# An S4 layer with MLP on one core: the tables of exponentials and sines built in one phase, or in two phases, one for each half of the channels

## The chip, the cores and the metric

The kernel runs on one core of one Trainium2 chip. It is written in Bass, with SBUF and PSUM addresses and the order of all instructions set by the kernel itself. The metric is the device time of one execution in microseconds (us). PE is TensorE, ACT is ScalarE, DVE is VectorE, POOL is GpSimd, and SP is the engine whose queue issues most of the DMAs.

## The reference

The input is u, 2048 positions by 512 channels, in bf16. An S4 layer with 128 complex states for each channel is followed by an MLP with 1376 hidden columns.

```python
# S4 part, on x = LN(u)
dt = exp(log_dt)[:, None]                      # 512 x 1
A, Bc, Cc = A_re + 1j*A_im, B_re + 1j*B_im, C_re + 1j*C_im   # 512 x 128
P = exp((dt*A)[:, :, None] * l)                # l = 0 .. 2047, rounded to bf16
K = einsum("dn,dnl,dn->dl", Cc, P, dt*Bc).real # one kernel of 2048 taps per channel
y = irfft(rfft(pad(x)) * rfft(pad(K)))[:2048] + x * Dskip
h = u + y
# MLP part
out = h + gelu_tanh(LN(LN(h)) @ w1 + b1) @ w2 + b2
```

The two layer norms in the MLP part are one in the launch's block and one in the MLP itself. All of the S4 part before the convolution (dt, A, K) depends on the parameters alone, and K needs a complex exponential for every channel, state and position.

## The kernel before, in words

**Tables.** The exponential of a position is split into a coarse and a fine part, so that K comes out of matrix products of tables with few entries per state. The table `EB`/`IB` has 33 entries (real and imaginary part) per state and channel, the table `EA`/`IA` 20. An entry is a gain (an exponential) times a cosine or a sine. The 512 channels are four chunks of 128 (`NCH`), two to a half: half 0 is chunks 0 and 1, half 1 chunks 2 and 3. For half 1 the A table stands in another layout, `EA2`/`IA2`.

**How an entry is made.** First the gain: `bexps` (L768 to L773, the Exp goes through L770) writes the gains of the B table straight from the exponent with 16 Exp of 1024 columns, all four chunks at once. `aexps` (L979 to L996) writes the gains of the A table: for each of five groups in each half, 16 small matmuls (L988) spread the exponent S3 into PSUM, and one Exp of 1024 columns reads it (L992 for half 0, L995 for half 1). Then the angle: `chain(hf, "B")` and `chain(hf, "A")` (L1020 to L1076) let PE accumulate the phase in PSUM (L1036, L1039, L1045, reading the phase S2), ScalarE takes the Sin of its low 16 bits (L1054, one for the sine and one for the cosine of four entries), and VectorE multiplies gains with sines and cosines (L1065 to L1067 and `product`, L1008 to L1015, a 2048-wide form; for half 1's A table two 1024-wide products, L1073 and L1074).

**S2, S3, S4.** The parameters are computed in the layout [state, channel]. The matmuls of the chains and of `aexps` want them in another one. `split` (L725) cuts each into a high and a low half, and `restack` (L729 to L734) moves them by DMAs of 32 KB through `dma` (L545), all on the SP queue: HLp and HLq (the phases) into S2, HLt and HLg (the exponent and the log gain) into S3, HLo (the offset of the angle) into S4. The log gain comes late: it needs complex products of the parameters on VectorE (L594), two squares and a Ln on ScalarE, and a cast on VectorE (L584).

**ScalarE's function table.** Exp and Ln are in one table, Sin and Arctan in another, Gelu in a third. `table()` (L526, L527) loads one. Before the change the order is: the table with Exp and Ln; all exponentials of both halves; the trigonometric table; the sines of half 0; small sines (`valB`, `T`, `TP`, `valD`, inputs of later products); the sines of half 1; much later the table with Gelu.

**What follows the tables.** `kgen` (L1083, matmuls L1098 and L1099) makes the taps of half 0, `kgen4` (L1115, matmuls L1129 and L1130) those of half 1; `carry` (L1141, L1146) and `kstage` (L1177) move them through DRAM into the layout of the transforms; `kspec` (L1169) and `xspec` (L942) transform taps and input; `inverse` (L1189, products at L1209 on VectorE, matmuls at L1219) transforms back, for the first and then the second half of the positions; `tail` (L1270) and `mlp` (L1330, matmuls L1342 and L1364, Gelu L1344) finish a quarter of the positions each. `stats` (L901) with the 16 `bn_stats` (L917) makes the mean and the deviation of the input's rows for `unorm` (L922), which the tail's first layer norm reads.

**What sets the order.** Each step is recorded by `add` with its engine, a planned cost and what it reads and writes. A written-out list, `ORDER`, then gives the order of all steps on all engines (a negative entry takes a step's second choice of engine). An engine does its steps in that order, whatever is ready behind them. Where the plan has PE idle for long, `run` (L297) puts filler matmuls in (`fill`, L1457 and L1458), which compute nothing that is used. Four PSUM tensors of 128 by 1024 f32 are handed from step to step.

Of the kernel before, what the change touches and what calls it, by code (L numbers as in the profile page):

```python
# [159 lines left out]
class VS(V):  # L160
# [246 lines left out]
def kernel(ctx, tc, A_u, A_A_re, A_A_im, A_B_re, A_B_im, A_C_re, A_C_im, A_log_dt, A_Dskip,  # L407
# [360 lines left out]
    def bexps(pr):  # L768
        for e0 in range(1, 17):
            add("ACT", c_act(1024) + 0.03, lambda e, e0=e0: act.activation(multi(EB0, BSZ, bf16, NCH, NB, CW)[:, :, 16 - e0:17 + e0:2 * e0, :].rearrange("p c k d -> p k c d"), th[0:4].ap().rearrange("p (k h) (c d) -> p k (h c) d", k=2, c=2), ACT.Exp, scale=float(8 * e0)),  # L770
                r=[th[0:4], TBL], w=[EB[c][16 + z * e0] for z in (1, -1) for c in range(NCH)], pr=pr + 0.01 * e0)
# [733 lines left out]
```

## Time and profile before

| | before |
|---|---|
| median of 3 runs | 251.6 us (250.97 to 251.65) |
| profiled execution | 251.55 us |
| its span in the trace | 249.8 us |
| granted TensorE clock, mean | 0.984 |
| PE busy, matmuls | 223.2 us, 89% of the span |
| weight loads (overlap PE) | 123.9 us, 50% |
| DVE busy | 175.5 us, 70% |
| ACT busy | 176.6 us, 71% |
| POOL busy | 24.1 us, 10% |
| DMA | 25.06 MB, mean 100 GB/s |

Views of the profile are used as follows. The 40 slices give each engine's busy share in tenths, one digit for 6.2 us. The table of stretches gives for each window its length, then the busy time and number of instructions of PE, weight loads, DVE, ACT and POOL, the mean granted clock, the DMA share and GB/s. A line of a timeline has the start, the busy time (of all instructions that the line groups), the engine, the source line, the operation with output and input, the number, and in brackets the idle time before it and what ended it. A line of the groups has busy time and mean length in ns, then the idle time before them.

### The profile page before, as it was taken

Reading aid. Unit: us, or ns where it says so; the run is one execution under the profiler, and the core shown is the slowest. Engines: PE = TensorE matmul, PEld = TensorE weight load, DVE = VectorE, ACT = ScalarE, POOL = GpSimd, SP = SyncE. Lnnn points to the kernel's source line nnn. Section 1 sums busy time; section 2 is a strip of 40 time slices with the busy share of each in tenths; the row PEclk is TensorE's granted clock in tenths of the full one; section 3 lists DMA queues with packets and bytes.
Section 4 is the critical chain, followed back from the end, with each engine's and each line's share of the span. In section 5 each row is a group of like instructions: output and inputs, shape, how many; then the busy total and the mean of one; then the engine's idle time right before and its main releaser. Section 6 shows DMA issues by size and latency. Waiting matters only on the chain.

```text
span 249.8 us, 7666 instructions
## 1 busy us (share of the span) xinstructions
PE 223.2 (89%) x3240; PEld 123.9 (50%) x3254; DVE 175.5 (70%) x355; ACT 176.6 (71%) x216; POOL 24.1 (10%) x208
## 2 busy tenths in 40 slices
PE   7264889978998999999998899999999999999993
PEld 3121643334676865344578555656544444444442
DVE  3999987999999475878999489964626947322022
ACT  3999997999999989979998539774613803703700
POOL 8665730000000000000000000000000000000000
PEclk9998599999999999999999999999999999999999
DMA  5583210100500208797688899704562042412112
GB/s 165 136 190 74 50 42 7 38 4 3 129 5 5 34 1 269 197 317 202 194 95 222 167 183 335 180 3 87 46 135 53 3 84 53 84 24 63 42 32 63
DMA packets 43203, 25.06 MB, mean 100 GB/s; under 512 B 27665, under 2 KB 40562, under 8 KB 43170
## 3 DMA queue, kind: packets, MB, share of 16 engines
q1 hardware_dynamic: 42578, 24.13, 41.0%
q10 hardware_dynamic: 592, 0.46, 0.7%
q8 instruction: 25, 0.41, 0.7%
q14 instruction: 8, 0.07, 0.1%
HBM read 10.03 MB, written 6.29 MB: 65 GB/s over the span
## 4 chain that ended last, share of the span: by engine, by line
PE 61%; ACT 23%; DVE 9%; issue 4%; POOL 0%; DVEq 0%; ACTq 0%; POOLq 0%
PE ps L1342 15%; PE ps L1364 15%; PE ps L1219 8%; ACT ar L770 6%; ACT ar L1054 6%; ACT ar L533 5%; PE ps L942 4%; PE ps L1169 3%; PE ps L1288 2%; PE ps L1458 2%; DVE ar L1015 2%; ACT ar L617 2%; PE ps L962 2%; PE ps L1129 2%; ACT ar L995 2%
## 5 line engine op out<-in xcount | busy, mean ns | idle before, releaser
L533 ACT CAST ar<-ps 128x1024 bf16<-128x1024 f32 (+3 forms) x75 | 66.6, 972 | 17.3 <-PE ps L1219 5.7
L1344 ACT ACTIVATE ar<-ps,ar 128x512 bf16<-128x512 f32 (+1 forms) x44 | 28.0, 686 | 35.2 <-PE ps L1342 27.7
L1364 PE MATMUL ps<-ar 128*128 128x512 bf16 (+3 forms) x181 | 39.3, 366 | 0.3
L1342 PE MATMUL ps<-ar 128*128 128x512 bf16 (+1 forms) x176 | 39.5, 379 | 0.0
L1209 DVE TENSOR_TENSOR ar<-ar 128x1024 bf16<-128x1024 bf16 x48 | 30.1, 686 | 10.3 <-PE ps L1219 9.8
L1366 DVE TENSOR_TENSOR ar<-ps,ar 128x512 bf16<-128x512 f32 (+1 forms) x17 | 11.0, 659 | 36.4 <-PE ps L1364 23.5
L1054 ACT ACTIVATE ar<-ps 128x1024 bf16<-128x1024 int16 x36 | 34.5, 1041 | 1.9 <-PE ps L1045 1.6
L535 DVE CAST ar<-ps 128x1024 bf16<-128x1024 f32 (+2 forms) x25 | 28.2, 1148 | 9.3 <-ACT ar L533 3.9
L1364 PEld LDWEIGHTS <-ar 128*128 128x128 bf16 (+1 forms) x187 | 18.0, 98 | 19.9 <-issue 0.4
L1342 PEld LDWEIGHTS <-ar 128*128 128x128 bf16 (+1 forms) x176 | 17.4, 100 | 20.3 <-issue 0.4
L1219 PE MATMUL ps<-ar 64*128 64x128 bf16 x768 | 23.8, 216 | 2.1 <-issue 1.2
L1045 PE MATMUL ps<-ar 128*32 128x256 f16 (+1 forms) x368 | 21.5, 331 | 4.2 <-ACT ar L1054 3.8
L1458 PE MATMUL ps<-ar 128*128 128x512 bf16 x72 | 20.9, 421 | 4.8 <-DMA ar<-in_A_u_dram 4.2
L1219 PEld LDWEIGHTS <-ar 64*128 64x128 bf16 x768 | 21.9, 94 | 6.3 <-issue 4.5
L962 PE MATMUL ps<-ar 128*32 128x512 bf16 (+1 forms) x320 | 17.5, 338 | 0.9 <-ACT ar L533 0.6
L1015 DVE TENSOR_TENSOR ar<-ar 128x2048 bf16<-128x2048 bf16 x14 | 16.9, 1230 | 1.1 <-ACT ar L1054 1.1
L1045 PEld LDWEIGHTS <-ar 128*32 128x32 f16 x368 | 9.5, 96 | 14.6 <-issue 11.7
L770 ACT ACTIVATE ar<-ar 128x1024 bf16<-128x1024 f32 x16 | 15.9, 1044 | 0.0
L942 PE MATMUL ps<-ar 128*32 128x512 bf16 x256 | 15.8, 380 | 0.0
L1458 PEld LDWEIGHTS <-ar 128*128 128x128 bf16 x79 | 7.7, 105 | 16.1 <-issue 10.5
L617 ACT ACTIVATE ar<-ar 128x512 f32<-128x512 f32 (+9 forms) x19 | 12.7, 677 | 1.7 <-DMA ar<-in_A_log_dt_dram 1.7
L988 PE MATMUL ps<-ar 128*32 128x256 f16 x160 | 8.0, 337 | 5.0 <-POOL ar L718 3.1
(104 smaller groups left out, 283.1 us busy)
## 6 DMA issues: line engine op xcount, KB each, us to landing
ar<-AK_d SPq DMA_DIRECT2D x8, 512.0 KB, 5.6
ar<-in_A_u_dram SPq DMA_DIRECT2D x4, 512.0 KB
AK_d<-ar SPq DMA_DIRECT2D x2, 1024.0 KB, 4.9
AK_d<-ar SPq DMA_DIRECT2D x4, 512.0 KB
out_dram<-ar SPq DMA_DIRECT2D x30, 64.0 KB, 2.1
ar<-in_B_w_dram SPq DMA_DIRECT2D x4, 344.0 KB, 5.1
ar<-ar SPq DMA_DIRECT2D x40, 32.0 KB, 1.9
ar<-in_B_w_dram SPq DMA_DIRECT2D x2, 640.0 KB
```

Of the source, the lines that this page charges most:

```text
L533: act.copy(out_fn(), in_fn())
L535: dve.tensor_copy(out_fn(), in_fn())
L770: add("ACT", c_act(1024) + 0.03, lambda e, e0=e0: act.activation(multi(EB0, BSZ, bf16, NCH, NB, CW)[:, :, 16 - e0:17 + e0:2 * e0, :].rearr ...
L942: pe.matmul(pst(p)[32 * cg:32 * cg + 32, 512 * z:512 * z + 512], lhsT=BD.ap()[:, 32 * f + 2 - 2 * jl:32 * f + 34 - 2 * jl], rhs=un[2 * (2 ...
L1045: pe.matmul(pst(p)[32 * g:32 * g + 32, 256 * j:256 * (j + n)].rearrange("p (a b) -> p a b", a=n), lhsT=W2[DELTAS.index(d)].ap(), rhs=S2[g] ...
L1054: add("ACT", c_act(1024), lambda e, o_=o_, i_=i_: act.activation(o_(), i_(), ACT.Sin, scale=SINSC), r=[p, TBL], w=[sc[cs]])
L1209: dve.tensor_tensor(o, a, b_[:, :, ::-1, :] if sw else b_, ALU.mult)
L1219: pe.matmul(pst(p)[:, 512 * h + 128 * k:512 * h + 128 * k + 128], lhsT=q.ap()[rows, 2 * k + r, :], rhs=TP[w].ap()[rows, f0 // 2 + k, :], s ...
L1342: pe.matmul(pst(p)[:fs, 512 * z:512 * z + 512], lhsT=w1s[dc].ap()[:, fc * P:fc * P + fs], rhs=ybuf.ap().rearrange("p (t c) k -> p c t k", ...
L1344: add("ACT", c_act(512, 1), lambda e, p=p, z=z, fc=fc, fs=fs: act.activation(hT.ap()[:fs, fc, :], pst(p)[:fs, 512 * z:512 * z + 512], ACT. ...
L1364: pe.matmul(pst(p)[:, 512 * z + c0:512 * z + c1], lhsT=hT.ap()[:fs, fc, 128 * t:128 * t + 128], rhs=w2s[fc].ap()[:fs, c0:c1], start=(fc == ...
L1458: pe.matmul(slots[z][:, 0:512], lhsT=identb.ap(), rhs=hs[15].ap(), start=True, stop=True)
```

## The change

`bexps` gets the half as a parameter and writes two chunks at a time: 16 Exp of 512 columns for half 0 and 16 for half 1 in place of 16 of 1024. `aexps` gets the half as well. The order on ScalarE becomes: exponentials of half 0, trigonometric table, the `TP` sines and the sines of half 0, table with Exp and Ln, the Ln and Exp of `stats`, the exponentials of half 1, trigonometric table, the sines `valB`, `T` and `valD`, the sines of half 1. So there are two more loads of the function table. The 2048-wide `product` of the A table of half 0 is replaced by the two 1024-wide products that half 1 had. `ORDER` is a new list, which also moves steps that the code does not: ten of the `bn_stats`, the memset of EA2's pads and three POOL products stand at other places or on another engine, and the fillers are 88 in place of 79.

```diff
--- before.py
+++ after.py
@@ -173,41 +173,43 @@
 LAG = {"PE": 0.19, "ACT": 0.20, "DVE": 0.14, "POOL": 0.15, "SP": 0.15}
 OWN = {"PE": 0.0, "ACT": 0.17, "DVE": 0.11, "POOL": 0.1, "SP": 0.0}
 ORDER = [
...
 ]
 
 
@@ -765,12 +767,12 @@
     add("DVE", c_dve(256, 1, True), th3, r=[p, dtb], w=[th[3]], hv=0)
     TT(th[4], p, dtb, ALU.mult, n=256, psum=True, oap=by4(th[4], 0, 256), aap=lambda pa=pa: pa()[:, 64:128], bap=by4(dtb, 256, 512), pr=0.42)
     CP(th[0:2], th[2:4], -1.0, n=512, pr=0.35)
-    def bexps(pr):
+    def bexps(hf, pr):
         for e0 in range(1, 17):
-            add("ACT", c_act(1024) + 0.03, lambda e, e0=e0: act.activation(multi(EB0, BSZ, bf16, NCH, NB, CW)[:, :, 16 - e0:17 + e0:2 * e0, :].rearrange("p c k d -> p k c d"), th[0:4].ap().rearrange("p (k h) (c d) -> p k (h c) d", k=2, c=2), ACT.Exp, scale=float(8 * e0)),
-                r=[th[0:4], TBL], w=[EB[c][16 + z * e0] for z in (1, -1) for c in range(NCH)], pr=pr + 0.01 * e0)
-
-    bexps(1.0)
+            add("ACT", c_act(512) + 0.03, lambda e, e0=e0: act.activation(multi(EB0 + 2 * hf * BSZ, BSZ, bf16, 2, NB, CW)[:, :, 16 - e0:17 + e0:2 * e0, :].rearrange("p c k d -> p k c d"), th[0:4].ap().rearrange("p (k h) (c d) -> p k h c d", k=2, c=2)[:, :, hf], ACT.Exp, scale=float(8 * e0)),
+                r=[th[hf], th[2 + hf], TBL], w=[EB[c][16 + z * e0] for z in (1, -1) for c in (2 * hf, 2 * hf + 1)], pr=pr + 0.01 * e0)
+
+    bexps(0, 1.0)
     S.pr = 0.4
     t2, t4 = tE(f32, 512), tE(f32, 512)
     gr, gi, sg = tE(f32, 512), tE(f32, 512), tE(f32, 512)
@@ -915,7 +917,6 @@
     S.pr = 1.2
     for s in range(16):
         add("DVE", c_dve(512) + 0.05, lambda e, s=s: dve.bn_stats(st[s].ap(), hs[s].ap()), r=[hs[s]], w=[st[s]], hv=0, pr=1.2 + 0.001 * (s // 4))
-    stats(st, nw, 16, 1.0, EPS, 1.25, ln=True)
     UN = [[X0s[j] for j in range(7)] + [at(zlo + 1024 * b, bf16, 512)] for b in range(2)]
 
     def unorm(b, pr):
@@ -976,24 +977,23 @@
     def dmaj(v, a):
         return v.ap().rearrange("p c g a i -> p (c g) a i")[:, :, a:a + 4, :]
 
-    def aexps(pr):
-
-        for hf in range(2):
-            for n in range(5):
-                p = Ps()
-
-                def fn(e, p=p, n=n, hf=hf):
-                    for j in range(4):
-                        for g in range(4):
-                            pe.matmul(pst(p)[32 * g:32 * g + 32, 256 * j:256 * j + 256], lhsT=W3[4 * n + j].ap(), rhs=S3[g].ap()[:, 256 * hf:256 * hf + 256], start=True, stop=True, tile_position=(0, 32 * g))
-                S.pr = pr + 0.1 * n + 0.5 * hf
-                add("PE", 0.45, fn, r=[W3, S3], w=[p], new=[p])
-                if hf == 0:
-                    add("ACT", c_act(1024), lambda e, p=p, n=n: act.activation(multi(E0 + 4 * n * 256, ASZ, bf16, 2, 4, CW).rearrange("p c a d -> p a c d"), pst(p).rearrange("p (a c d) -> p a c d", a=4, c=2), ACT.Exp),
-                        r=[p, TBL], w=[EA[c][4 * n + z] for c in range(2) for z in range(4)])
-                else:
-                    add("ACT", c_act(1024), lambda e, p=p, n=n: act.activation(dmaj(EA2, 4 * n).rearrange("p x a i -> p a x i"), pst(p).rearrange("p (a x i) -> p a x i", a=4, x=8), ACT.Exp),
-                        r=[p, TBL], w=[EA2])
+    def aexps(hf, pr):
+
+        for n in range(5):
+            p = Ps()
+
+            def fn(e, p=p, n=n, hf=hf):
+                for j in range(4):
+                    for g in range(4):
+                        pe.matmul(pst(p)[32 * g:32 * g + 32, 256 * j:256 * j + 256], lhsT=W3[4 * n + j].ap(), rhs=S3[g].ap()[:, 256 * hf:256 * hf + 256], start=True, stop=True, tile_position=(0, 32 * g))
+            S.pr = pr + 0.1 * n
+            add("PE", 0.45, fn, r=[W3, S3], w=[p], new=[p])
+            if hf == 0:
+                add("ACT", c_act(1024), lambda e, p=p, n=n: act.activation(multi(E0 + 4 * n * 256, ASZ, bf16, 2, 4, CW).rearrange("p c a d -> p a c d"), pst(p).rearrange("p (a c d) -> p a c d", a=4, c=2), ACT.Exp),
+                    r=[p, TBL], w=[EA[c][4 * n + z] for c in range(2) for z in range(4)])
+            else:
+                add("ACT", c_act(1024), lambda e, p=p, n=n: act.activation(dmaj(EA2, 4 * n).rearrange("p x a i -> p a x i"), pst(p).rearrange("p (a x i) -> p a x i", a=4, x=8), ACT.Exp),
+                    r=[p, TBL], w=[EA2])
 
     nch = [0]
 
@@ -1069,13 +1069,8 @@
             else:
                 e0, i0, q, lo = E0, BA0, ASZ, b0 * 256
             rE, rI = regs(e0, q, lo, 4), regs(i0, q, lo, 4)
-            if hf:
-                add("DVE", c_dve(1024, 2), lambda e, lo=lo, Sx=Sx, e0=e0, i0=i0, q=q: dve.tensor_tensor(ent(i0, q, lo, 4), ent(e0, q, lo, 4), Sx(), ALU.mult), r=rE + [sc[0]], w=rI)
-                add("DVE", c_dve(1024, 2), lambda e, lo=lo, Cx=Cx, e0=e0, q=q: dve.tensor_tensor(ent(e0, q, lo, 4), ent(e0, q, lo, 4), Cx(), ALU.mult), r=rE + [sc[1]], w=rE + mark)
-                continue
-            product(lambda e0=e0, q=q, lo=lo: both(e0, q, lo, 4), lambda o: o[:, 1], sc, rE + [sc], rE + rI + mark)
-
-
+            add("DVE", c_dve(1024, 2), lambda e, lo=lo, Sx=Sx, e0=e0, i0=i0, q=q: dve.tensor_tensor(ent(i0, q, lo, 4), ent(e0, q, lo, 4), Sx(), ALU.mult), r=rE + [sc[0]], w=rI)
+            add("DVE", c_dve(1024, 2), lambda e, lo=lo, Cx=Cx, e0=e0, q=q: dve.tensor_tensor(ent(e0, q, lo, 4), ent(e0, q, lo, 4), Cx(), ALU.mult), r=rE + [sc[1]], w=rE + mark)
 
 
     KIS = [[(0, 11), (11, 11)], [(22, 10)]]
@@ -1374,7 +1369,7 @@
     pads = lambda v: v.ap().rearrange("p c g a i -> p (c g) a i")[:, :, NA:32, :]
     add("DVE", 1.0, lambda e: dve.memset(pads(EA2), 0.0), w=[EA2], pr=0)
     load_small()
-    aexps(0.95)
+    aexps(0, 0.95)
     table("trig_and_small")
     S.pr = 1.3
     at_ = gi
@@ -1395,19 +1390,24 @@
     PD(1.1, 0.62, lambda g: g.tensor_tensor(Jk.ap(), Jt.ap().unsqueeze(1).to_broadcast([P, 8, 64]), sk.ap().unsqueeze(2).to_broadcast([P, 8, 64]), ALU.mult), r=[Jt, sk], w=[Jk], pr=1.8, hv=6)
     for r in range(2):
         PTS(TPc, Jk, 1.0, 16384.0 * (1 - r), op1=ALU.add, n=512, oap=lambda r=r: TPc.ap().rearrange("p k (j r) -> p k j r", r=2)[:, :, :, r], pr=1.81)
-    chain(0, "B", 2)
-    chain(0, "A", 2.5)
-    AC(valB, codB, ACT.Sin, scale=SINSC, oap=lambda: valB.ap().rearrange("p a b -> p (a b)"), iap=lambda: low16(codB), tbl=True, pr=2.94)
-    bdo = lambda r: BD.ap()[:, 2:514].rearrange("p (f s q) -> p f s q", f=16, q=4)[:, :, :, r]
-    for r in range(2):
-        PD(0.6, 0.22, lambda g, r=r: g.tensor_tensor(bdo(r), valB[r].ap().unsqueeze(2).to_broadcast([P, 16, 8]), mB.ap().unsqueeze(1).to_broadcast([P, 16, 8]), ALU.mult), r=[valB, mB], w=[BD], pr=3.2, hv=6)
-    AC(T, codT, ACT.Sin, n=2048, scale=SINSC, oap=lambda: T.ap().rearrange("p a b c -> p (a b c)"), iap=lambda: low16(codT), tbl=True, pr=2.98)
     tpv = lambda v, r: v.rearrange("p (n r) -> p n r", r=2)[:, :, r]
     tpo = lambda n: TP[n].ap().rearrange("p a b -> p (a b)")
     for n, sc in enumerate((SINSC, -SINSC)):
         AC(TP[n], TPc, ACT.Sin, scale=sc, oap=lambda n=n: tpo(n), iap=lambda: low16(TPc), tbl=True, pr=2.96 + 0.003 * n)
     for r, sc in enumerate((-SINSC, SINSC)):
         AC(TP[2], TPc, ACT.Sin, n=512, scale=sc, oap=lambda r=r: tpv(tpo(2), r), iap=lambda r=r: tpv(low16(TPc), 1 - r), tbl=True, pr=2.966)
+    chain(0, "B", 2)
+    chain(0, "A", 2.5)
+    table("natural_log_exp_and_others")
+    stats(st, nw, 16, 1.0, EPS, 2.6, ln=True)
+    bexps(1, 2.7)
+    aexps(1, 2.8)
+    table("trig_and_small")
+    AC(valB, codB, ACT.Sin, scale=SINSC, oap=lambda: valB.ap().rearrange("p a b -> p (a b)"), iap=lambda: low16(codB), tbl=True, pr=2.94)
+    bdo = lambda r: BD.ap()[:, 2:514].rearrange("p (f s q) -> p f s q", f=16, q=4)[:, :, :, r]
+    for r in range(2):
+        PD(0.6, 0.22, lambda g, r=r: g.tensor_tensor(bdo(r), valB[r].ap().unsqueeze(2).to_broadcast([P, 16, 8]), mB.ap().unsqueeze(1).to_broadcast([P, 16, 8]), ALU.mult), r=[valB, mB], w=[BD], pr=3.2, hv=6)
+    AC(T, codT, ACT.Sin, n=2048, scale=SINSC, oap=lambda: T.ap().rearrange("p a b c -> p (a b c)"), iap=lambda: low16(codT), tbl=True, pr=2.98)
     AC(valD, codD, ACT.Sin, scale=SINSC, oap=lambda: valD.ap().rearrange("p a b -> p (a b)"), iap=lambda: low16(codD), tbl=True, pr=2.95)
     for g in range(4):
         PTS(DD, valD, mD[g:g + 1], n=32, oap=lambda g=g: DD.ap()[:, :, :, g], pr=4.5)
```

72 rows, old and new, of the table ORDER are left out of this document.

## The prediction

> **What bounds the kernel now.** I read the page's busy shares and 40 slices first, then the table of stretches, then the timelines of ScalarE, VectorE and the SP queue up to 80 us, because the change lies there.
>
> ```profile
> PE 223.2 (89%) x3240; PEld 123.9 (50%) x3254; DVE 175.5 (70%) x355; ACT 176.6 (71%) x216; POOL 24.1 (10%) x208
> PE   7264889978998999999998899999999999999993
> DVE  3999987999999475878999489964626947322022
> ACT  3999997999999989979998539774613803703700
> ...
> 20.00:40.00 20.00, 14.50 (x215) 7.80 (x214) 17.67 (x47) 19.98 (x26) 9.92 (x18) 0.83 0.17 41
> 40.00:60.00 20.00, 16.98 (x241) 7.07 (x241) 19.41 (x31) 18.49 (x24) 0.00 (x0) 1.00 0.06 15
> 60.00:80.00 20.00, 18.24 (x671) 13.46 (x664) 19.30 (x35) 19.66 (x24) 0.00 (x0) 1.00 0.18 43
> 80.00:122.00 42.00, 40.91 (x708) 22.89 (x700) 31.55 (x43) 38.00 (x42) 0.52 (x1) 1.00 0.59 175
> 122.00:160.00 38.00, 35.28 (x816) 25.07 (x809) 32.86 (x66) 29.32 (x34) 0.00 (x0) 1.00 0.88 185
> ...
> L1458 PE MATMUL ps<-ar 128*128 128x512 bf16 x24 | 6.2, 380 | 0.2
> ```
>
> PE's 89% is an average over two regimes. Up to 80 us ScalarE works 19.98, 18.49 and 19.66 us of each 20 and VectorE nearly as much: the kernel builds its tables of exponentials and sines, and PE waits and runs filler matmuls (L1458). From 80 us on PE is the bound: 40.91 of 42 us, and 35.28 of 38 in the stretch of the inverse transforms, 6.2 of them filler (24 matmuls). So the time is the moment at which the tables of half 1 are complete, plus a PE tail of nearly fixed length.
>
> ```profile
> 75.46 3.78 ACT L1054 ACTIVATE ar<-ps 128x1024 bf16<-128x1024 int16 x4 [0.19 <-PE ps L1045]
> 79.28 1.22 DVE L1015 TENSOR_TENSOR ar<-ar 128x2048 bf16<-128x2048 bf16 x1 [0.53 <-ACT ar L1054]
> 80.56 0.29 PE L1129 MATMUL ps<-ar 128*128 128x132 bf16 x1 [0.33 <-DVE ar L1015]
> ```
>
> That moment: the last sine ends at 79.24, the last product at 80.50, and the first kernel-tap matmul of half 1 (L1129, which reads all of them) starts at 80.56. It stays in place in the changed order, behind the last product. The profiled run took 251.55, span 249.8; the tail is 249.8 - 80.56 = 169.2, and 1.75 lies outside the span. The median of the runs is 251.6, so the two can be compared directly.
>
> **The change on ScalarE's own queue.** Both orders give, between the first Exp of the table (L770) and the last sine, the same sines, casts and exponentials, with two differences: 32 Exp of 512 columns instead of 16 of 1024, and two more table loads.
>
> ```profile
> 7.32 4.84 ACT L770 ACTIVATE ar<-ar 128x1024 bf16<-128x1024 f32 x5
> 12.07 0.99 ACT L533 COPY ar<-ps 128x1024 bf16<-128x1024 bf16 x1
> 16.33 1.14 ACT L617 ACTIVATE ar<-ar 128x512 f32<-128x512 f32 x2
> 33.15 1.95 ACT L992 ACTIVATE ar<-ps 128x1024 bf16<-128x1024 f32 x2
> 36.97 0.26 ACT L617 ACTIVATE ar<-ar 128x16 f32<-128x16 f32 x1
> 37.23 1.28 ACT L527 ACT_TABLE_LOAD   x1
> 46.20 1.07 ACT L617 ACTIVATE ar<-ar 128x1024 bf16<-128x1024 int16 x1
> 50.79 14.03 ACT L1054 ACTIVATE ar<-ps 128x1024 bf16<-128x1024 int16 x15
> ```
>
> Rows overlap by about 0.1, so an Exp of 1024 steps by (4.84 - 0.1)/5 = 0.95 and a 512-wide op by 0.52. No half-width Exp of this layout is in the trace; it lies between 0.475 (half of 0.95) and 0.57 (half of the 1.14 row), and I take 0.52. 32 x 0.52 - 16 x 0.95 = +1.4. A load takes 1.28 and starts at 37.23, exactly where the op before it ends (36.97 + 0.26), so the overlap of 0.1 is lost too: 1.38 each, +2.8 for two. Together +4.2. The Trainium skill (ScalarE: Activation LUTs, What ACT_TABLE_LOAD costs) gives 1283 ns for the load and a drain of about 1380 ns beside it, and its rule is to do all of one set before switching. The trace agrees on the load and shows no such drain; with it the sum would be about 2.7 higher.
>
> On VectorE nine 2048-wide products become pairs of 1024.
>
> ```profile
> 43.21 1.29 DVE L1065 TENSOR_TENSOR ar<-ar 128x1024 bf16<-128x1024 bf16 x2
> 46.36 1.22 DVE L1015 TENSOR_TENSOR ar<-ar 128x2048 bf16<-128x2048 bf16 x1
> ```
>
> A pair steps 1.2 (1.29 - 0.09) against 1.13: 9 x 0.07 = 0.6. At nothing, since in half 0 ScalarE needs 1.86 for two sines per pair. If VectorE were the later one it would cost that 0.6.
>
> Steps that only change place:
>
> ```profile
> L917 DVE BATCH_NORM_STATS2 ar<-ar 128x6 f32<-128x512 bf16 x16 | 9.8, 674 | 0.0
> L1375 DVE MEMSET ar<- 128x1536 uint32 x1 | 1.3, 1338 | 0.3 <-issue 0.3
> L718 POOL TENSOR_TENSOR ar<-ar 128x640 f16<-128x640 f32 x1 | 1.3, 1255 | 0.0
> ```
>
> Ten of the sixteen statistics go behind half 0's products on VectorE, 10 x 0.6 us, into the time in which ScalarE does the exponentials of half 1 and VectorE has little else; their Ln and Exp go with them, and what reads them (L928, L930) is needed only in the tail. The memset of EA2's pads (1.34) moves from the start into half 0's products. Three POOL products (L718 and two like it) go to VectorE, some 0.75 each (0.6 per 512 columns, by the products quoted next), ahead of 27 us where VectorE waits anyway. All at nothing; where that cover fails, VectorE's chain and so the switch are later by as much.
>
> **The change in time: when half 0 can start.** Before, the switch stood at 37.23, with ScalarE busy throughout. Three things must be there, and none is made by ScalarE alone.
>
> ```profile
> 13.09 2.49 DVE L594 TENSOR_TENSOR ar<-ps,ar 128x512 f32<-128x512 bf16 x4
> 20.13 0.62 DVE L584 TENSOR_SCALAR ar<-ar 128x512 f32<-128x512 f32 x2
> 20.24 13.72 SPq L545 DMA_DIRECT2D ar<-ar  x21
> 34.69 12.75 SPq L545 DMA_DIRECT2D ar<-ar  x10
> ar<-ar SPq DMA_DIRECT2D x40, 32.0 KB, 1.9
> 26.49 5.64 PE L988 MATMUL ps<-ar 128*32 128x256 f16 x125 [0.23 <-DMA ar<-ar]
> 27.73 1.01 ACT L995 ACTIVATE ar<-ps 128x1024 bf16<-128x1024 f32 x1
> 36.80 1.01 PE L1045 MATMUL ps<-ar 128*32 128x256 f16 x16
> 39.19 1.00 ACT L1054 ACTIVATE ar<-ps 128x1024 bf16<-128x1024 int16 x1
> ```
>
> (a) VectorE's complex products start at 13.09 and lead, over two squares and a Ln on ScalarE, to the cast of the log gain at 20.13 (L584). In the changed order the same VectorE work stands ahead of them, so they start at 13.05 again; a 672-wide product now stands between. I get the cast at 19.75, give or take 1. (b) Only then can the SP queue issue the gain's restack copies, at 13.72/21 = 0.65 each: eight copies, 1.9 to landing, so S3 is complete at 19.75 + 7 x 0.65 + 1.9 = 26.2, as before (the matmuls of L988 flow from 26.49). Before, ScalarE reached these tables at 27.73 and never noticed. Now its queue up to there holds 16 Exp at 0.52, the cast of 0.95 and eight 512-wide ops, 13.4 us, which would end at 20.7; it waits 6.3 us in all, on VectorE and then on S3: first aexps at 27.0, with 0.8 for 16 matmuls at the pace of the x125 row and the hand-over. Five of them at 0.93, the load 1.38 and the arctan 0.52 end at 33.5. (c) The sines need S2, whose last copy is the 20th behind the gain's first (by the built order 12 of the 32 copies for S2 and S3 stand ahead of the gain's; it was the 23rd: 21 and the first two of the x10 row): 19.75 + 19 x 0.65 + 1.9 = 34.0, plus the 0.8. First sine of half 0 at 34.8 against 39.19: 4.4 us earlier, not the 7 + 4.6 that the removed ScalarE work suggests.
>
> **The sum.** Half 0: 18 sines at 0.93, two 1024-wide at 0.95, two 512-wide at 0.52, one of 0.2: 19.9, so ScalarE is free at 54.7. Before, half 0 lasted from 39.19 to the tenth sine of the x15 row, 50.79 + 10 x 0.93 = 60.1, thus 20.9. VectorE's products follow to about 57 and cover nothing that ScalarE now waits for. Then what was done ahead of 37 comes due: load 1.38, 16 Exp 8.3, five aexps 4.65, Ln and Exp of the statistics 0.3, load 1.38, two small sines 0.3, and 0.8 that I give for an aexp whose matmuls stand behind kernel-tap matmuls of half 0 on PE: 17.1, to 71.8. Half 1 took 79.24 - 60.1 = 19.1 with one 1024-wide sine that is now earlier: 18.2, last sine at 90.0, last product and hand-over 1.3 later as before. L1129 starts at 91.3 instead of 80.56: +10.7.
>
> PE uses the wait: all kernel-tap matmuls of half 0 (L1098, L1099) fit ahead of it, but they did so before (the last ones end at 80.5). New ahead of it are two kspec groups of half 0.
>
> ```profile
> 86.52 1.04 PE L1169 MATMUL ps<-ar 20*128 20x512 bf16 x16
> ```
>
> 16 matmuls step 0.97, two groups -1.9; a third (narrow, about 0.55) moves behind the first inverse transforms, where filler stands: -0.6. Spill, carry copies and reload of half 0 on the SP queue come earlier relative to the tail, which feeds PE no work that it lacks. The tail is otherwise the same 161.9 us of PE work. 251.55 + 10.7 - 2.5 = 259.75, say 259.8.
>
> Unseen: the first table load now stands ahead of log_dt's DMA on ScalarE's queue.
>
> ```profile
> 4.64 0.63 ACT L617 ACTIVATE ar<-ar 128x512 bf16<-128x512 bf16 x1 [1.70 <-DMA ar<-in_A_log_dt_dram]
> 4.65 0.33 ACTq L545 DMA_DIRECT2D ar<-in_A_B_re_dram  x1
> ```
>
> A DMA issue behind an ACTIVATE started 0.01 after that began, so the queue runs ahead of the engine: 0. If it waits the load out, everything above is 1.3 later. A gain is excluded: the products at 13.05 wait for VectorE, not for the inputs. The bounds on the cast's time (1 us each way) and on the half-width Exp (-1.4 to +1.6 over 32) carry straight to the end.
>
> **The rivals.** *ScalarE is not starved* (0.10): the SP copies and VectorE's chain run early enough for ScalarE to do its queue without waiting. Then L1129 moves by the +4.2 of own work alone and the time is 251.55 + 4.2 - 2.5 = 253.3. For it: ScalarE is 19.98 of 20 busy where I see the waits. Against: S2 and S3 landed only just in time even before (36.80, 26.49).
>
> *A drain at each switch* (0.05): two further loads each cost as much again, 2 x 1.28: 262.3. Against it speaks the row at 37.23. The Trainium skill's page on ScalarE gives this cost, as said.
>
> *The tail shrinks: faster* (0.09). Half 0's taps are spilled and reloaded earlier relative to half 1, the DMA crowd (share 0.88 in 122:160) thins, and PE loses its idle there: 42 - 40.91 + 38 - 35.28 = 3.8, and 6.2 of filler, 10.0 in all. With all of it gone: 249.8. It decides from 8.2 recovered on (259.75 - 251.55). Against: those waits are on VectorE's products and the casts of the inverse stage, which are all still there.
>
> **How the numbers follow.** What a measurement can tell from no change is 0.3%, 0.75 us. Forecast with starvation 0.76, at 259.8, own range 256.5 to 263.5: 1 us for the cast, 1.3 for the first load, and 3 us of tail either way, a third of the 10.0 above. The range takes in the rivals without starvation and with a drain: 253.0 to 264.0. Faster needs the third rival: 0.07, and the part of it that just reaches no change 0.02; slower is the rest, 0.91.
>
> **What would show it.** In the new profile: first sine (L1054) at 34 to 36; idle of ScalarE between 13 and 34 of some 6 us, ended by VectorE and by PE matmuls that wait for DMAs; three loads of 1.28 within 5 and 72; the matmuls of L1129 (L1124 in the new file) from 90 to 93; from there to the end 165 to 169. Wrong would be: L1124 before 87 (starvation overrated), a first sine before 33, gaps of over 1 us around the loads, or a tail under 161.

## The result, and the profile after

The changed kernel takes 260.52 us (median of 3 runs, 260.52 to 260.73) against 251.6; the ratio is 1.0365, 95% interval 1.0329 to 1.0402. Its profiled execution took 260.52 with a span of 258.7, that of before 251.55 with 249.8: 8.9 longer inside the span, and the rest outside it as before.

On the page of the changed kernel PE is busy for 87% of the span and ScalarE for 70% (89% and 71% before). ScalarE's row of the 40 slices (6.5 us each) is:

```profile
ACT  2975759999999998999899758876321734803710
```

ScalarE has digits of 5 and 7 in the slices from 13 to 39 us, where the slices of the kernel before have a 9 up to 37 us. Its timeline, with the idle time ahead of a row and what ended it in brackets, from the first Exps to the first sine, and below it the rows that open and close each later phase:

```profile
7.42 3.75 ACT L772 ACTIVATE ar<-ar 128x512 bf16<-128x512 f32 x7
...
15.76 1.23 ACT L619 ACTIVATE ar<-ar 128x512 f32<-128x512 f32 x2 [0.56 <-DVE ar L596]
17.75 0.72 ACT L619 ACTIVATE ar<-ar 128x512 f32<-128x512 f32 x1 [0.76 <-DVE ar L596]
21.02 0.63 ACT L604 ACTIVATE ar<-ar 128x512 f16<-128x512 f32 x1 [0.99 <-DVE ar L596]
24.65 1.38 ACT L619 ACTIVATE ar<-ar 128x512 f32<-128x512 f32 x2 [1.96 <-DVE ar L596]
27.52 4.69 ACT L992 ACTIVATE ar<-ps 128x1024 bf16<-128x1024 f32 x5 [1.48 <-PE ps L988]
32.22 1.28 ACT L529 ACT_TABLE_LOAD   x1
33.52 0.63 ACT L619 ACTIVATE ar<-ar 128x512 f32<-128x512 f32 x1
36.86 1.02 ACT L1054 ACTIVATE ar<-ps 128x1024 bf16<-128x1024 int16 x1 [2.72 <-PE ps L1045]
...
41.97 1.94 ACT L1054 ACTIVATE ar<-ps 128x1024 bf16<-128x1024 int16 x2 [0.44 <-PE ps L1045]
...
57.72 1.28 ACT L529 ACT_TABLE_LOAD   x1
59.02 1.70 ACT L772 ACTIVATE ar<-ar 128x512 bf16<-128x512 f32 x3
...
72.60 1.28 ACT L529 ACT_TABLE_LOAD   x1
74.16 3.77 ACT L1054 ACTIVATE ar<-ps 128x1024 bf16<-128x1024 int16 x4
...
79.66 12.17 ACT L1054 ACTIVATE ar<-ps 128x1024 bf16<-128x1024 int16 x13
```

The last sine ends at 91.83 instead of 79.24. The table of stretches from the first Exp of the B table to the last sine (length, busy time and count of PE, weight loads, DVE, ACT and POOL, then the granted clock, the DMA share and GB/s) says what that is made of. The first row is the kernel before, the second the changed one:

```profile
7.32:79.24 71.92, 55.17 (x1090) 30.26 (x1097) 67.97 (x138) 70.05 (x85) 17.47 (x125) 0.95 0.24 56
7.42:91.83 84.41, 57.71 (x1163) 30.89 (x1161) 74.85 (x152) 75.29 (x103) 11.02 (x74) 0.98 0.22 50
```

The stretch is 12.5 longer. 5.2 of it is ScalarE's own work (18 more instructions: 16 Exps and two loads), 7.3 is waiting (84.41 - 75.29 = 9.1 against 71.92 - 70.05 = 1.9).

PE gives part of it back. Its rows in the changed kernel; then, for the first kernel-tap matmul of half 1 and the first matmul of the inverse transforms, the rows that give the first and the last start of a line:

```profile
26.73 2.49 PE L988 MATMUL ps<-ar 128*32 128x256 f16 x80 [0.57 <-DMA ar<-ar]
35.52 1.30 PE L1045 MATMUL ps<-ar 128*32 128x256 f16 x15 [3.33 <-DMA ar<-ar]
90.60 1.04 PE L1164 MATMUL ps<-ar 20*128 20x512 bf16 x16
92.11 1.04 PE L1164 MATMUL ps<-ar 20*128 20x512 bf16 x16
93.14 0.29 PE L1124 MATMUL ps<-ar 128*128 128x132 bf16 x1
...
L1214 PE MATMUL ps<-ar x768: 213/216/227, 131.3 to 188.8; 64*128 64x128 bf16 x192
```

```profile
L1219 PE MATMUL ps<-ar x768: 213/216/227, 122.4 to 179.9; 64*128 64x128 bf16 x192
```

The kernel taps start at 93.14 instead of 80.56, 12.6 later. From them to the inverse transforms it is 131.3 - 93.1 = 38.1, before 122.4 - 80.6 = 41.8; from there to the end it is 127.4 in both. So the tail is 165.6 instead of 169.2, and all of the difference lies ahead of the inverse transforms. In the table of stretches, this part before and after:

```profile
80.56:122.40 41.84, 41.08 (x696) 22.83 (x696) 31.39 (x43) 37.84 (x43) 0.52 (x1) 1.00 0.60 177
93.14:131.30 38.16, 37.92 (x657) 23.16 (x655) 32.11 (x45) 34.99 (x40) 0.52 (x1) 1.00 0.57 174
```

PE's idle time in it goes from 0.76 to 0.24; the other 3.2 of the 3.7 is less PE work.

### The profile page after: what moved, and what is told of

It is laid out like the page before. It is cut to its first block, busy times and chain, and to the rows that moved or that the text cites. A ratio compares the mean times of both kernels' runs of the same rounds, so it can differ in the third digit from the quotient of the medians.

```text
span 258.7 us, 7726 instructions
## 1 busy us (share of the span) xinstructions
PE 224.5 (87%) x3263; PEld 124.4 (48%) x3263; DVE 182.3 (70%) x375; ACT 180.8 (70%) x232; POOL 18.0 (7%) x199
## 4 chain that ended last, share of the span: by engine, by line
PE 57%; ACT 18%; DVE 10%; DMA 5%; issue 3%; SPq 3%; POOL 2%; ACTq 0%; DVEq 0%; POOLq 0%
PE ps L1337 15%; PE ps L1359 15%; PE ps L1214 8%; ACT ar L1054 8%; PE ps L943 4%; ACT ar L772 3%; DVE ar L596 3%; ACT ar L535 3%; DMA ar<-AK_d 3%; PE ps L963 3%; SPq L547 3%; PE ps L1458 3%; PE ps L1045 2%; PE ps L1164 2%; PE ps L1124 2%
## 5 line engine op out<-in xcount | busy, mean ns | idle before, releaser
L535 ACT CAST ar<-ps 128x1024 bf16<-128x1024 f32 (+3 forms) x73 | 65.0, 958 | 16.1 <-PE ps L1214 5.5
L1339 ACT ACTIVATE ar<-ps,ar 128x512 bf16<-128x512 f32 (+1 forms) x44 | 28.8, 686 | 28.7 <-PE ps L1337 18.5
L1359 PE MATMUL ps<-ar 128*128 128x512 bf16 (+3 forms) x187 | 39.9, 367 | 0.0
L1458 PE MATMUL ps<-ar 128*128 128x512 bf16 x88 | 23.7, 407 | 13.8 <-DMA ar<-in_A_u_dram 13.1
L537 DVE CAST ar<-ps 128x1024 bf16<-128x1024 f32 (+3 forms) x27 | 30.9, 1156 | 5.9 <-PE ps L943 2.1
L1045 PE MATMUL ps<-ar 128*32 128x512 f16 (+1 forms) x368 | 22.8, 346 | 8.8 <-ACT ar L1054 5.2
L772 ACT ACTIVATE ar<-ar 128x512 bf16<-128x512 f32 x32 | 18.3, 632 | 0.0
L596 DVE TENSOR_TENSOR ar<-ar 128x4 f32<-128x4 f32 (+9 forms) x44 | 12.7, 304 | 3.9 <-POOL ar L665 3.2
L612 DVE SCALAR_TENSOR_TENSOR ar<-ar 128x4 f32<-128x4 f32 (+4 forms) x44 | 11.3, 264 | 3.1 <-ACT ar L619 2.1
```

The source lines that it names most:

```text
L535: act.copy(out_fn(), in_fn())
L537: dve.tensor_copy(out_fn(), in_fn())
L772: add("ACT", c_act(512) + 0.03, lambda e, e0=e0: act.activation(multi(EB0 + 2 * hf * BSZ, BSZ, bf16, 2, NB, CW)[:, :, 16 - e0:17 + e0:2 * ...
L1045: pe.matmul(pst(p)[32 * g:32 * g + 32, 256 * j:256 * (j + n)].rearrange("p (a b) -> p a b", a=n), lhsT=W2[DELTAS.index(d)].ap(), rhs=S2[g] ...
L1339: add("ACT", c_act(512, 1), lambda e, p=p, z=z, fc=fc, fs=fs: act.activation(hT.ap()[:fs, fc, :], pst(p)[:fs, 512 * z:512 * z + 512], ACT. ...
L1359: pe.matmul(pst(p)[:, 512 * z + c0:512 * z + c1], lhsT=hT.ap()[:fs, fc, 128 * t:128 * t + 128], rhs=w2s[fc].ap()[:fs, c0:c1], start=(fc == ...
```

## The experiments

The theory under test: ScalarE's waits in the first phase, for VectorE's chain and for the restack copies, make up most of the loss; the work of half 1 that used to fill them now stands behind. The rivals: the loads cost more than their rows show; half 1's exponentials cover other work, so that nothing is lost by them. Each kernel ran beside the kernel before, and each ratio is to that. In the diffs a line with # puts the new ORDER into words, and "..." stands for code left out.

**Two loads alone**, in the kernel before:

```diff
+    for name in ("natural_log_exp_and_others", "trig_and_small"):
+        add("ACT", 1.3, lambda e, name=name: act.preload_act_table_set(name))
     chain(1, "B", 4)
```

> The kernel before, with two more loads of ScalarE's function table (the one with Exp, then the trigonometric one) between the sines of half 0 and those of half 1; nothing else is moved. What two loads cost by themselves: if each is its 1.28 us and the lost overlap of 0.1, the first kernel-tap matmul of half 1 goes from 80.56 to 83.3 and the time to 251.6 + 2.8 = 254.4. If each load also drains ScalarE for as long again, 256.9. If the loads were the main cost of the change (its 8.9, and the 3.7 that the tail gave back), some 264.

Measured: 253.5 against 251.53, ratio 1.0077 (1.0050 to 1.0104), so +1.9 (1.3 to 2.6). ScalarE's timeline and PE's first kernel tap:

```profile
60.06 2.57 ACT L1434 ACT_TABLE_LOAD   x2
62.64 4.83 ACT L1068 ACTIVATE ar<-ps 128x1024 bf16<-128x1024 int16 x5
...
L1143 PE MATMUL ps<-ar x64: 217/226/292, 83.2 to 93.8; 128*128 128x132 bf16 x64
```

Two loads take 2.57, the sine follows at once, and the kernel taps start 2.6 later (83.2 against 80.56). The span is only 1.2 longer (251.0 against 249.8), for the tail is 251.0 - 83.2 = 167.8, 1.4 less than before. ScalarE loses no further time beside the loads, and they are not the main cost.

**The B table's Exps back in the first phase, full width:**

```diff
-    bexps(0, 1.0)
+    bexps(1.0)          # 16 of 1024 columns, both halves
...
-    bexps(1, 2.7)
```

> The changed kernel with the Exps of the B table as before: 16 of 1024 columns for both halves, all in the first phase; the Exps of the A table of half 1 stay in the second, with both loads. Theory of starvation: the 6.9 us of extra work in the first phase go into ScalarE's waits there (5.8 between 13 and 27.5, and 2.7 ahead of the first sine, which stays near 36.9), and the second phase loses 8.3. First kernel-tap matmul of half 1 at 84.8, time 260.5 - 8.3 = 252.2, up to 3.7 more if the tail loses what it had won. Rival, ScalarE's own work sets the end in both phases: only the width counts, -1.4, 259.1.

Measured: 262.05, ratio 1.0426 (1.0377 to 1.0474). Both figures were missed. ScalarE's and VectorE's rows:

```profile
14.07 0.99 ACT L548 COPY ar<-ps 128x1024 bf16<-128x1024 bf16 x1
15.09 2.48 DVE L609 TENSOR_TENSOR ar<-ps,ar 128x512 f32<-128x512 bf16 x4 [2.35 <-ACT ar L548]
31.15 4.69 ACT L1005 ACTIVATE ar<-ps 128x1024 bf16<-128x1024 f32 x5 [0.75 <-PE ps L1001]
39.69 1.02 ACT L1067 ACTIVATE ar<-ps 128x1024 bf16<-128x1024 int16 x1 [1.91 <-PE ps L1058]
...
67.89 1.95 ACT L1008 ACTIVATE ar<-ps 128x1024 bf16<-128x1024 f32 x2 [2.78 <-PE ps L1001]
```

The copy out of PSUM (L548) stands on ScalarE behind seven of the Exps, now twice as long: it went from 11.07 to 14.07. VectorE's complex products wait for it, and the whole chain to the first aexps and the first sine is some 3 later. I had filled the waits from the wrong side, ahead of the instruction that they hang on. In the second phase ScalarE then waited for the matmuls of aexps, which stand behind half 0's kernel taps on PE.

**Six of the late phase copies on ScalarE's queue:**

```diff
-dma("SP", lambda dst=dst: dst.ap(), ...
+dma("ACT" if S is S2 and (rb, w, g) in LATE else "SP", lambda dst=dst: dst.ap(), ...
```

> The changed kernel with six of the restack copies of the phase (S2) that stand last on the SP queue issued by ScalarE's queue, behind the last Exp of half 0's B table, where ScalarE waits. If the SP queue is what the first sine waits for: S2 lands at some 30.5 instead of 35.5, ScalarE then goes from the arctan (34.2) almost straight to the first sine, 34.4 instead of 36.9, and the time is 260.5 - 2.5 = 258.0. If the copies only stood beside another wait: 260.5, or later by the time that six issues take on ScalarE, up to 2.7 (263.2).

Measured: 260.63, ratio 1.0376 (1.0316 to 1.0436): no gain. ScalarE's rows, and a row of the SP queue's waits (total, times, longest):

```profile
29.90 4.69 ACT L1008 ACTIVATE ar<-ps 128x1024 bf16<-128x1024 f32 x5 [3.55 <-PE ps L1004]
36.44 1.01 ACT L1070 ACTIVATE ar<-ps 128x1024 bf16<-128x1024 int16 x1
...
SPq L561 <- DMA ar<-in_A_u_dram: 3.3, 3, 1.8
```

The wait ahead of the first sine is gone, as the theory says of S2. But the SP queue now waited 3.3 for loads of the input ahead of the gain's copies (in the changed kernel 0.8, between the gain's second copy and its third), the first aexps came 2.4 later, and the sine hardly earlier.

**The HLt copies on ScalarE's queue instead**, four HLp copies ahead of the gain's:

```diff
-    restack(HLt, 0, 0.43, S3)
+    restack(HLt, 0, 0.43, S3, "ACT")
```

> The changed kernel with the eight restack copies of HLt issued by ScalarE's queue, between the first Exps, and the four last HLp copies moved ahead of the gain's on the SP queue, so that only 8 of the 16 phase copies are left behind the gain's. If the SP queue's 0.63 a copy is what the first sine waits for: the last phase copy is issued at 29.1 instead of 33.5, the first sine follows the arctan at 34.4 instead of 36.9, and the time is 258.0. If the gain's copies come later instead, as when six phase copies went to ScalarE's queue, the first aexps is later than 27.5 by as much and the time stays at 260.5.

Measured: 262.88, ratio 1.0432 (1.0391 to 1.0473), a miss by both accounts. ScalarE's waits and rows:

```profile
ACT ar L786 <- DMA ar<-in_A_u_dram: 3.3, 2, 1.8
...
13.56 0.99 ACT L549 COPY ar<-ps 128x1024 bf16<-128x1024 bf16 x1
38.29 1.00 ACT L1068 ACTIVATE ar<-ps 128x1024 bf16<-128x1024 int16 x1
```

Now the issues on ScalarE waited for the input's loads, and its Exps and the PSUM copy with them (13.56 instead of 11.07). Again no wait is left ahead of the first sine, and now the chain through VectorE is later. In both runs the edit made S3 with the gain later (first aexps at 29.90 and 31.76 against 27.52), so that ScalarE itself came late to the first sine. That S2's copies set the first sine of the changed kernel rests on PE's row at 35.52, which waited 3.33 for a DMA; what an earlier S2 alone would give these two runs do not show.

**Half 1's Exps in ScalarE's waits.** Three steps led here. First, the 16 half-width Exps were put behind the instructions that others wait for (one ahead of the Squares and one behind them, two, four and three in the next waits, five ahead of the load):

```diff
     bexps(0, 1.0)
+    bexps(1, 1.0)
...
-    bexps(1, 2.7)
 # order on ScalarE: the Exps of half 1 spread over its waits between 15 and 34 us;
 # on PE: aexps and the first phase matmuls of half 1 ahead of half 0's kernel taps
```

> The changed kernel with the 16 half-width Exps of half 1's B table put into ScalarE's waits of the first phase (11 between 15 and 27.5, five between the last Exp of half 0's A table and the table load), each behind the instruction that others wait for; in the second phase the matmuls of aexps and of the first sines of half 1 stand ahead of half 0's kernel taps on PE, and the statistics are spread over VectorE's waits. Theory of starvation: the first sine stays near 36.9, the second phase loses 8.3, the first kernel-tap matmul of half 1 is at 84.6 (93.1 in the changed kernel). The time is 252.2, up to 3.7 more where PE has no room left for the work that it did in the wait. Rival, that half 1's exponentials only cover another chain (VectorE's products and half 0's kernel taps on PE) and the end stays where it is: 258 or more.

Measured: 263.77, ratio 1.0483 (1.0442 to 1.0524). ScalarE's rows:

```profile
36.59 1.01 ACT L1069 ACTIVATE ar<-ps 128x1024 bf16<-128x1024 int16 x1
...
42.81 3.77 ACT L1069 ACTIVATE ar<-ps 128x1024 bf16<-128x1024 int16 x4 [3.60 <-PE ps L1060]
...
69.61 1.93 ACT L1069 ACTIVATE ar<-ps 128x1024 bf16<-128x1024 int16 x2
78.82 1.96 ACT L1069 ACTIVATE ar<-ps 128x1024 bf16<-128x1024 int16 x2 [7.28 <-PE ps L1060]
```

The first sine stands at 36.59 (36.86 in the changed kernel) with all 16 Exps done ahead of it: 8.3 us of work cost nothing there. This is the most direct sign that ScalarE was starved in the first phase. The time was lost behind it, in two waits for PE that my order had made: 16 fillers that the kernel put ahead of half 0's phase matmuls, and half 0's kernel taps ahead of half 1's phase matmuls. The second step took both away:

```diff
-... and fs:
+... and fs and i not in NOFILL:      # no fillers up to half 1's kernel taps
 # order on PE: half 0's kernel taps in pieces between half 1's phase matmuls
```

> As the run that put half 1's 16 half-width Exps into ScalarE's waits, with the two new waits of that run taken away: no fillers on PE up to half 1's kernel taps (16 of them, 4.4 us, stood ahead of the chain's matmuls at 37.8), and half 0's kernel taps in pieces between the phase matmuls of half 1 instead of all ahead of them (a wait of 7.3 for ScalarE). Theory of starvation: first sine at 36.6, half 0's sines done at 57.5, the second phase 8.0 instead of 16.4, first kernel-tap matmul of half 1 at 84.6 to 86, time 252 if the tail keeps what it won in the changed kernel, 255.5 if not. Rival, that PE's half 0 work needs the time that half 1's exponentials took: 258 or more, with ScalarE waiting for PE between 65 and 85.

Measured: 268.21, ratio 1.0645 (1.0570 to 1.0719): slower still. ScalarE's rows:

```profile
66.87 1.92 ACT L1070 ACTIVATE ar<-ps 128x1024 bf16<-128x1024 int16 x2
...
79.76 1.02 ACT L1070 ACTIVATE ar<-ps 128x1024 bf16<-128x1024 int16 x1 [6.35 <-DVE ar L1088]
```

The first sine of half 1 came at 66.87 (74.16 in the changed kernel; the forecast makes it 57.5 + 8.0 = 65.5), but then VectorE, whose queue I had left with small steps and kernel-tap casts ahead of half 1's products, held the sines up. The third step uses the order of the kernel before for everything from half 1's sines on, and beside it ran the changed kernel with that same order, so that the two differ up to half 1's sines alone: in the filled waits, the fillers, and the places of the statistics and of aexps' matmuls:

```diff
 # order: the steps up to the second trigonometric load as in the run before;
-# all later steps: the changed kernel's order
+# all later steps: the order of the kernel before
```

> As the run before it (half 1's 16 half-width Exps in ScalarE's waits, no fillers up to half 1's kernel taps), but from half 1's sines on all engines have the order of the kernel before, in which ScalarE did not wait there. Theory of starvation: first sine at 36.9, first sine of half 1 at 66.9 as in that run (74.2 in the changed kernel), half 1 as long as in the kernel before without the sine that is now earlier (19.5), first kernel-tap matmul of half 1 at 86.4 (93.1). With the tail of the kernel before (169.2) the time is 257.3; 256 if a later start is partly made good, as the run with two loads showed (1.3). Rival, that something else than ScalarE's work holds half 1 up: first kernel-tap matmul at 92 or later, time 263 or more.

> The changed kernel in both phases, but from half 1's sines on all engines have the order of the kernel before, with its kspec groups behind half 1's kernel taps. Theory that the tail is shorter because PE work was moved into the wait: first kernel-tap matmul of half 1 at 93 as in the changed kernel, the tail 169.2 (167.9 with the 1.3 that a later start gives), time 262.8 to 264.2. Rival, that the tail is shorter because half 0 is ready earlier, whatever the order: 260.5 or less.

Measured: 260.21 with the waits filled (ratio 1.0334, 1.0292 to 1.0375), 264.87 without (1.0541, 1.0501 to 1.0581). First sines of half 1 on ScalarE, a stretch of 10 us (the figure ahead of the last two is the granted clock), and the kernel taps on PE, with filled waits:

```profile
66.87 4.79 ACT L1070 ACTIVATE ar<-ps 128x1024 bf16<-128x1024 int16 x5
...
40.00:50.00 10.00, 7.94 (x87) 3.46 (x88) 9.97 (x19) 8.51 (x11) 0.00 (x0) 0.52 0.18 28
...
L1140 PE MATMUL ps<-ar x64: 219/226/293, 89.8 to 100.4; 128*128 128x132 bf16 x64
```

and without:

```profile
73.64 4.80 ACT L1068 ACTIVATE ar<-ps 128x1024 bf16<-128x1024 int16 x5
...
L1138 PE MATMUL ps<-ar x64: 218/224/294, 94.9 to 105.6; 128*128 128x132 bf16 x64
```

Filling the waits brings half 1's first sine 6.8 earlier, its kernel taps 5.1 and the end 4.7 (264.87 - 260.21). That is the theory, with less than the 8.3 of work that was moved: half 0 and half 1 both ran slower than forecast, ScalarE waiting again for VectorE, and with the fillers gone PE's clock was 0.52 between 40 and 50 (1.00 there in the changed kernel). Since the fillers and some places differ as well, the 4.7 cannot be put down to the Exps alone. With the waits filled the time is still 8.5 above the kernel before (260.21 against 251.75): the loads and the five Exps of half 1's A table (4.69 at 60.17) stand in the second phase as in the changed kernel, and no run takes the rest apart. The tails are 258.9 - 89.8 = 169.1 and 264.4 - 94.9 = 169.5, that of the kernel before (169.2): the shorter tail belongs to the changed order of the late steps, not to the phases. That order as a whole is worth 4.4 (264.87 without it, 260.52 with it).

**The two kspec groups put back**, in the changed kernel:

```diff
-# PE: kspec, kspec | kernel taps of half 1
+# PE: first half of the kernel taps | kspec, kspec | the rest
```

> The changed kernel with the two kspec groups of half 0 that stand ahead of half 1's kernel taps put back behind the first half of them, where they stood before. Theory that the tail is shorter by PE work that was done in the wait: these two groups come back, 2 x 0.97: 262.4. If the tail is shorter for another reason (fewer waits, other order): 260.5, within 0.5.

> The two kspec groups put back behind the first half of half 1's taps as in the run before, but without fillers between half 1's taps (there were 10 in that run, 3.6 us of PE, and none in the changed kernel). If the groups cost their own PE time: 260.5 + 1.9 = 262.4. If PE then waits there for PSUM space that ScalarE and VectorE have to empty, and the fillers only stood in that wait: 266, as with them.

Measured: 266.54 with fillers (ratio 1.0608, 1.0557 to 1.0660), 266.8 without (1.0602, 1.0567 to 1.0637), both +6 where 1.9 was forecast. Of the first, two rows of fillers; then rows and stretches of the second:

```profile
97.91 0.59 PE L1472 MATMUL ps<-ar 128*128 128x512 bf16 x2
99.52 1.47 PE L1472 MATMUL ps<-ar 128*128 128x512 bf16 x6
```

```profile
93.88 0.29 PE L1139 MATMUL ps<-ar 128*128 128x132 bf16 x1 [2.48 <-DVE ar L1030]
...
101.82 1.04 PE L1179 MATMUL ps<-ar 20*128 20x512 bf16 x14 [0.90 <-ACT ar L550]
...
102.00:104.00 2.00, 2.00 (x25) 1.44 (x18) 1.04 (x1) 1.99 (x3) 0.00 (x0) 0.68 0.00 0
104.00:106.00 2.00, 2.00 (x21) 2.00 (x19) 1.30 (x3) 0.93 (x2) 0.00 (x0) 0.50 0.39 133
```

With the fillers PE worked through and spent 2.1 on the eight of these rows; without them it waited 0.9 there for a cast, and the granted clock then fell to 0.5. The time without fillers fits its second account (266, a wait for PSUM space that the fillers only covered), but the trace shows just this 0.9 of such a wait, and the clock beside it. So these two runs do not say what the groups cost by themselves, and the run with the old order says only what the late order costs as a whole.

## Why the prediction was right

It forecast 259.8 (own range 256.5 to 263.5) and slower; measured 260.52. The mechanism held; that the total is only 0.7 off is in part luck, since two terms missed by more than 1 us in opposite directions. By its steps:

- **Bound and switch point.** Right: the kernel taps of half 1 stay behind the last product and 1.3 behind the last sine (91.83 to 93.14), and PE's work follows them with 0.24 of idle time up to the inverse transforms. The forecast put them at 91.3.
- **Half-width Exps and loads.** Seven Exps take 3.75: (3.75 - 0.1)/7 = 0.52 as assumed. A load steps 1.30 (32.22 to 33.52, 57.72 to 59.02), against 1.38 with the lost overlap. The Trainium skill (ScalarE: Activation LUTs, What ACT_TABLE_LOAD costs) has a drain of about 1380 ns with each switch. Neither the three loads here, whose next rows start 0.01 to 0.02 behind their ends, nor the two alone (2.57) show it. ScalarE's added work in all was 5.2, not 4.2. No run takes the excess apart; an estimate is that the five more waits, each with the 0.1 of overlap that a row behind a wait loses, are 0.5 of it.
- **The first load, ahead of log_dt's DMA.** Rightly put at 0: the load starts at 0.73, the issue at 0.77, and the first Exp of the table at 7.42 instead of 7.32.
- **Steps that only change place.** At nothing, and VectorE's chain was indeed not later. Two readings were wrong without harm. The cast that the gain's copies wait for is not the f32 row at 20.13 (L584) but the f16 row ahead of it (L604, 19.78 to 20.21 before; L606, 19.23 to 19.66 after), with the first copy at 20.24 and 19.68 (forecast 19.75). And by the groups of both profiles five POOL products went to VectorE, not three, and two others went to POOL.
- **Starvation.** Right in mechanism: ScalarE waited four times for VectorE and once for aexps' matmuls, 5.75 between 13 and 27.5 (6.3 forecast). Filling these waits brought 4.7 us, fillers and places included. The first aexps came at 27.52 (27.0).
- **First sine, the step that was mis-sized.** 36.86 instead of 34.8. The forecast let the SP queue issue a copy every 0.65. The SP queue's rows for the gain's first copy and the one that follows 18 copies later (start, time to the end of the group, copies left in it):

```profile
19.68 22.53 SPq L547 DMA_DIRECT2D ar<-ar  x28
32.90 9.32 SPq L547 DMA_DIRECT2D ar<-ar  x10
```

  18 steps take 13.2, 0.73 each: most are 0.63, but two are 1.45 (20.23 to 21.68, with a wait of 0.8 for a load of the input) and 1.80 (28.56 to 30.36, cause not shown). That is 1.5 of the 2.1. The rest is PE's phase matmuls behind the landing: after 3.3 us of idleness 15 of them took 1.30 at 35.52, at a granted clock of 0.66, where 16 took 1.01 before.
- **Half 0, second phase, half 1.** 20.9 (19.9), 16.4 (17.1), 17.7 (18.2). The 0.8 for an aexp behind kernel taps on PE did not occur; 0.4 of half 0's excess was a wait for phase matmuls (at 41.97).
- **The tail.** -3.7 instead of -2.5. Three full kspec groups (0.97 each, 2.9) are gone from the stretch up to the inverse transforms, where two and a narrow one were counted, and 0.5 is PE idleness that the stretch lost; the last 0.3 stays open. The PE work of the old tail is 161.6 from 80.56 on; the forecast's 161.9 begins at 80. The two misses, +1.8 at the kernel taps and -1.2 here, nearly cancel.
- **Rivals.** "Not starved" (253.3) fell with the waits; "a drain at each switch" fell with the two loads alone; "the tail shrinks" needed 8.2 beyond the 2.5 that the forecast already took off, and got 1.2, ahead of the inverse transforms and not in the crowded stretch that it named: from there to the end it is 127.4 in both.
- **Signs and range.** ScalarE's idle time and the tail (165.6) came out as named. The first sine (36.86 instead of 34 to 36), the third load (72.60 instead of by 72) and the kernel taps (93.14 instead of 90 to 93) were just later than named, the last two largely by the first sine's delay. None of the signs of being wrong appeared. The range is narrower than the sum of its three bounds (1 + 1.3 + 3 = 5.3), and the forecast does not say why.

## What to carry to other kernels

When work is moved behind a function-table switch, price first what it used to cover: here two loads and narrower instructions cost about 5, and the uncovered waits 7. A wait in front of an engine is to be filled behind the instruction that others wait for; work put ahead of it delayed the very chain that the wait hangs on, here by 3. A forecast with several terms should be judged by its terms, since two of them missed by over 1 us with opposite signs.

## What the runs showed of the hardware that was not expected

A DMA issue on ScalarE's queue can stall its arithmetic: with eight copies there, the Exps behind them waited 3.3 by the profile for loads of the input, and 1.0 for other copies. In the run with six copies the first two issues (21.02 and 21.66) passed beside running activations.

PE's granted clock fell to 0.5 some 10 us after a wait of 2.5 and right behind one of 0.9: in the second kspec run, without fillers, PE waited 2.5 ahead of half 1's taps (93.88) and 0.9 ahead of the row at 101.82, and the clock was 0.68 from 102 to 104 and 0.50 from 104 to 106. With the fillers it was 1.00 there. What exactly makes it fall is not shown. The Trainium skill (TensorE: Matmul & The Clock Gate, Part 1) names half rate as the state after an idle window of about 3.4 us. The rate agrees, but in the 12 us ahead of the fall no single wait is that long.
